# Attention and two MLPs on one core: program order on three engines before the first up product

## The chip, the core and the metric

One core of a Trainium2 chip runs the whole program. The time is device microseconds (us) of one execution; what counts is the median over several runs. TensorE (PE in the profile; PEld is its weight load), VectorE (DVE), ScalarE (ACT), GpSimd (POOL) and the DMA queues (SP and ACT issue on hardware queues, POOL on a software queue) each work through an instruction stream of their own, in order, and wait for one another by semaphores.

## What is computed

```python
def _attn_ref(q, k, v, s):                      # q, k, v: (4, 8, 576, 64); s: (4, 8, 576)
    scores = 1.0 / np.sqrt(D) * np.matmul(q, k.transpose(0, 1, 3, 2))
    cum = np.cumsum(np.maximum(s, 0.0), axis=-1)
    bias = -(cum[:, :, :, None] - cum[:, :, None, :])
    scores = np.where(causal, -1000000000.0, scores + np.minimum(bias, 0.0))
    attn = np.exp(scores - np.max(scores, axis=-1, keepdims=True))
    attn = attn / (np.sum(attn, axis=-1, keepdims=True) + 1e-09)
    return np.matmul(attn, v)
def reference(...):
    x = _attn_ref(q, k, v, s)                   # -> (2304, 512), all heads side by side
    x = np.maximum(x @ moe_w_in, 0.0) ** 2 @ moe_w_out          # 512 -> 2048 -> 512
    h = x @ moe2_w_in
    return np.maximum(0.01 * h, h) @ moe2_w_out
```

## The kernel before

The attention takes its 32 heads two at a time: 16 pairs, x = 0 to 15. A pair is worked in seven steps, k = 0 to 6, and the program's loop (line 810) counts them all as y = 7x + k. STEPS says what a step is: kind 0 (rows 0 to 255 of one head) at k = 0 and 1, kind 2 at k = 2 and 3, kind 3 at k = 4 and 5, kind 4 (the last 64 rows of both heads) at k = 6.

For one step the work goes through the engines in turn. TensorE makes the scores (`scores`, lines 457 and 469), two blocks ahead. VectorE adds the mask and takes the row's maximum (`maxima`, line 488). ScalarE makes the exponentials and their sums (`exponentials`, line 512). One or two steps later TensorE turns them (`flip`, line 527), and the turned blocks are copied out of PSUM by ScalarE (kinds 0 and 2, line 550) or by VectorE (kinds 3 and 4, line 548). TensorE multiplies them with v (`values`, line 569): the first 256 rows at k = 5, the rest at k = 3 of the next pair. ScalarE copies the product (`gather`, line 579).

The division by the sums comes in two portions for the first five pairs. `inverse` (lines 585 to 589) adds 1e-9 and takes the reciprocal on VectorE, and GpSimd spreads it over a tile `ex`; `spread` (line 604) turns that on TensorE; `scale` (lines 610 and 614) multiplies on VectorE. With k0 counted from the pair's own first step, the first portion has its inverse at k0 = 5 and its product at 9, the second its inverse at 8 and its product at 12.

Beside that, jobs come at fixed steps (`at_slot`): `load_bias`, `turn` (VectorE's transposes of the next pair's k and q, lines 427 and 430; from pair 5 on also a high and a low part, on ScalarE, line 431, and GpSimd, line 432), `last_rows` (GpSimd), `load_qk` (eight DMAs for two pairs, line 389), `load_v` (three DMAs and a GpSimd memset, lines 402 to 407), the loads of the attention's output as x of the first MLP (`up1_x`, with `split`: line 617 on ScalarE, line 618 on VectorE), and from step 11 on `load_w`: it reads 16 chunks of the first weight matrix (line 154, two `wst` buffers), each of which three steps later is put together from two words per element by ScalarE (lines 114 and 115), one step after that by VectorE (117 and 120) and GpSimd (122), then rounded by ScalarE (169) with the rest taken by GpSimd (172).

START[0] is step 35, the start of pair 5. From there on the first MLP's up products (`up1`, line 661) are laid between the attention's steps, and TensorE has enough to do. The ramp is what lies before: five pairs of attention alone. After the attention come the second half of the first MLP and the second MLP (line 877).

What sets the order. The program is written as one list of instructions. A planner then gives each engine its own order: it takes the instruction that is ready soonest by its own estimate, and the one written earlier among those that are ready. `in_order(start, engines)` (line 316) takes that freedom away: it chains what was written since `start` on each of the engines named, so that the engine works in the written order. `after(i)` (line 308) only says that what is written inside, on the engine of i, stands behind i in that engine's stream. Before the change TensorE alone is chained, from step 35 on (lines 812 and 871), and in the ramp only within each step (line 840). VectorE and ScalarE are free everywhere.

Of the kernel before, what the change touches and what calls it, by code (L numbers as in the profile page):

```python
# [23 lines left out]
def attention_then_two_mlps(  # L24
# [24 lines left out]
    nc = tc.nc  # L49
# [258 lines left out]
    def after(*instructions):  # L308

        stack = ExitStack()  # L310
        for i in instructions:
            if i is not None:
                stack.enter_context(tc.issue_after(i))
        return stack

    def in_order(start, engines):

        before = {}
        for i in nc.cur_bb.bb.instructions[start:]:
            if i.engine not in engines:  # L320
                continue
            if i.engine in before:
                tc.add_manual_dep(
                    i, before[i.engine].name,
                    mybir.DependencyInfo(mybir.DependencyClass.NoSync, mybir.DependencyReason.DATA),
                    reason="in_order")
            before[i.engine] = i
# [146 lines left out]
    def maxima(at, x, kind, e):  # L474

        p = pairs[x]  # L480
        if kind == 3 and x < PLAIN:
            t = f32(p.Y[:, 3 * e])
        else:
            t = at.tile([P, S], F32, tag="t", name="t", bufs=TB)
        m = at.tile([P, 16], F32, tag="m", name="m", bufs=TB + 1)

        def reduce(sc, msk, a, z, first, m):
            return nc.vector.tensor_tensor_reduce(t[:, a:z], sc, msk, -QK_SCALE, first, ALU.add, ALU.min, m).ins  # L488

        sc = p.sc[kind][e]  # L490
        if kind == 0:
            tiles = ((0, P, 0), (P, 3 * P, 1))
            for a, z, c in tiles:
                done = reduce(sc[:, a:z], mask[:, S - z + a:], a, z, 3.0e38, m[:, c:c + 1])
        elif kind == 4:
            tiles = ((0, S, 0),)
            reduce(sc[:, :S // 2], mask[:, :S // 2], 0, S // 2, 3.0e38, m[:, 1:2])
            done = reduce(p.sc[kind][1][:, :S // 2], mask4, S // 2, S, m[:, 1:2], m[:, 0:1])
        else:
            tiles = ((0, (kind + 1) * P, 0),)  # L500
            done = reduce(sc[:, :(kind + 1) * P], mask[:, S - (kind + 1) * P:], 0, (kind + 1) * P, 3.0e38, m[:, 0:1])
        if kind == 0 and e == 0:
            p.sums = at.tile([P, 16], F32, tag="sums", name="sums", bufs=4)
        T = {0: 0, 2: 2, 3: 3, 4: 4}[kind]
        p.t = t
        return t, m, tiles, p.sums, 2 * T + e, done

    def exponentials(t, m, tiles, sums, c0):

        for x, (a, z, c) in enumerate(tiles):  # L510
            s0 = c0 + 2 * x
            done = nc.scalar.activation(t[:, a:z], t[:, a:z], AF.Exp, bias=m[:, c:c + 1], scale=-1.0,  # L512
                                        accum_out=sums[:, s0:s0 + 1])
        return done.ins
# [59 lines left out]
    def gather(at, x, region, po):  # L574

        p = pairs[x]
        if region == 0:
            p.xo = at.tile([P, S], F32, tag="xo", name="xo", bufs=2)
        nc.scalar.activation(p.xo[:, :R] if region == 0 else p.xo[:, R:], po, AF.Copy)

    def inverse(at, x, a, z):

        p = pairs[x]
        cols = p.sums[:, 2 * a:min(2 * z, 9)]
        nc.vector.tensor_scalar(cols, cols, 1.0e-9, None, ALU.add)
        nc.vector.reciprocal(cols, cols)
        w = 2 * (min(z, 4) - a)
        p.ex = at.tile([P, w, 64], F32, tag="ex", name="ex")
        nc.gpsimd.tensor_copy(p.ex, p.sums[:, 2 * a:2 * a + w].unsqueeze(2).to_broadcast([P, w, 64]))
# [81 lines left out]
    def attention(at, mg, mx):  # L671

        n = len(STEPS)
        end = n * len(pairs)
        later = {}

        def at_slot(y, f, *args):
            later.setdefault(y, []).append((f, args))
# [58 lines left out]
        for x in range(len(pairs)):  # L737
            y = n * x
            if x + 1 < len(pairs):
                if x:  # L740
                    at_slot(y, load_bias, x + 1)
                late = 2 if x <= PLAIN else 0
                at_slot(y + 1 + late, turn, at, x + 1, "k")
                at_slot(y + 2 + late, turn, at, x + 1, "q")
                at_slot(y + 5, last_rows, x + 1)
            if x + 2 < len(pairs):
                if x and x % 2 == 0:
                    at_slot(y + 3, load_qk, at, x + 2)
                at_slot(y + 5, load_v, at, x + 2)

        def store(x):
            p = pairs[x]
            for e in range(2):
                c, d0 = divmod(p.h[e] * D, P)
                nc.sync.dma_start(xscr[c, d0:d0 + D, p.b * S:(p.b + 1) * S], p.xo[64 * e:64 * e + 64])
# [12 lines left out]
        def values_at(x, region):  # L768

            return 10 if region or ALONE <= x < len(pairs) - 1 else 5 if x < ALONE else 6  # L770
# [38 lines left out]
        live, anchors = {}, [None, None]  # L809
        for y in range(end + 14):  # L810
            x, st = divmod(y, n)
            if y == START[0]:
                fixed_from = len(nc.cur_bb.bb.instructions)
            if y < end:
                args = maxima(at, x, *STEPS[st])
                live[y] = args[0]
                behind = [args[-1], exponentials(*args[:-1])]
            fill(y, 0)
            tiled = len(nc.cur_bb.bb.instructions)
            for early in (True, False):  # L820
                for px in (x - 1, x):
                    if early or not 0 <= px < len(pairs):
                        continue
                    k0 = y - n * px
                    for region in range(2):
                        if k0 == values_at(px, region):
                            pairs[px].po[region] = values(px, region)
                for z in (y - LAG, y - 1):
                    zx, zs = divmod(z, n)
                    kind, e = STEPS[zs]  # L830
                    if early != (kind == 0 and zx < ALONE):
                        continue
                    if 0 <= z < end and (e or kind == 4) and (z == y - 1) == (kind == 3 and zx >= ALONE):
                        flip(at, zx, kind, [live.pop(i) for i in range(z - e, z + 1)])
            if y + 1 < end and STEPS[(y + 1) % n][1] == 0:
                last = len(KINDS) * x + KINDS.index(STEPS[st][0])
                while asked <= last + (2 if last + 2 < AHEAD else 1):
                    scores(asked // len(KINDS), KINDS[asked % len(KINDS)])
                    asked += 1
            in_order(tiled, (nc.tensor.engine,))  # L840
            divided = [i for i in nc.cur_bb.bb.instructions[tiled:] if i.engine == nc.tensor.engine][-1:]
            for px in (x - 1, x):
                if not 0 <= px < len(pairs):
                    continue
                k0 = y - n * px
                for region in range(2):
                    if k0 == values_at(px, region) + (region or px >= ALONE):
                        gather(at, px, region, pairs[px].po[region])
                final = 12 if px < ALONE else 13
                portions = ((9, 0, 2), (final, 2, 5)) if px < ALONE else ((final, 0, 5),)  # L850
                for when, a, b in portions:
                    if k0 == when:
                        scale(px, a, b)
                    if k0 == when - 4:
                        inverse(at, px, a, b)
                    if k0 == when - 1:
                        spread(px, a, b)
                if k0 == final:
                    store(px)
            with after(*divided):  # L860
                fill(y, 1)
            with after(*anchors, raw["last"]):
                for f, args in later.pop(y, ()):
                    f(*args)
            if y < end:
                anchors = behind
            fill(y, 2)
# [238 lines left out]
    with ExitStack() as stack:  # L1106
        b = open_pools(stack, ("b10", "bp2", "bp1", "bwst", "b00", "b01", "bop0", "bop1", "b11", "bwt"))
# [11 lines left out]
    with ExitStack() as stack:  # L1119
        b = open_pools(stack, ("c62", "cpa", "cpb", "cwst", "c17", "cy", "c543", "cp2", "cwa", "cwt"))  # L1120
# [17 lines left out]
    with ExitStack() as stack:  # L1138
        b = open_pools(stack, ("d01", "dpost", "dturn", "dpad", "dop0", "d00", "d11", "d10", "dop1"))
# [35 lines left out]
```

## Time and profile before

| | us |
|---|---|
| median of 3 runs (930.95 to 931.68) | 931.44 |
| the profiled execution | 932.79 |
| its span, first to last instruction | 931.0 |
| TensorE busy | 898.3 (96%) |
| VectorE busy | 705.7 (76%) |
| ScalarE busy | 577.7 (62%) |
| GpSimd busy | 179.9 (19%) |
| first up product (line 661) starts | 78.70 |

How to read it: a row of a timeline gives the start in the span, the length, engine, line, operation, output<-inputs, shape, and in brackets how long the engine had stood idle before and what ended that. [...] The profiled execution is 932.79 us long and its span 931.0, so 1.8 us lie around the span.

### The profile page before, as it was taken

What the parts mean: (1) busy time and instruction counts of PE and PEld (TensorE: products, weight loads), DVE (VectorE), ACT (ScalarE), POOL (GpSimd) and SP (SyncE); (2) the same over time, 40 slices, a digit from 0 to 9 for tenths busy, and PEclk for the clock granted to TensorE, in tenths of its full rate; (3) what the DMA queues carried; (4) which work ended last, traced back from release to release, by engine and by line L of the source; (5) the groups of instructions that cost most, each with busy time, mean ns of one, the idle gap of its engine ahead of it and who ended that gap; (6) DMA issues with size and microseconds to landing.
All of it is one profiled execution on the core that took longest, in us unless ns stands there. A gap on an engine that the chain in (4) does not pass through costs nothing.

```text
span 931.0 us, 16390 instructions
## 1 busy us (share of the span) xinstructions
PE 898.3 (96%) x5902; PEld 809.0 (87%) x5902; DVE 705.7 (76%) x1286; ACT 577.7 (62%) x1076; POOL 179.9 (19%) x290
## 2 busy tenths in 40 slices
PE   5878999999999999999999999999999999999997
PEld 3646777777777778999999999999999999999997
DVE  5888776876774267589897997787488697886964
ACT  4788876878886444365565556686577754444442
POOL 4357763344330001001112101001110000000000
PEclk9999999999999999999999999999999999999999
DMA  9776849778763377948649326668768575627303
GB/s 164 172 184 153 217 145 230 219 204 245 227 203 106 99 239 274 316 163 269 228 132 363 128 96 201 218 221 304 256 205 299 187 254 149 182 57 208 86 13 55
DMA packets 229569, 178.48 MB, mean 192 GB/s; under 512 B 139600, under 2 KB 206352, under 8 KB 229488
## 3 DMA queue, kind: packets, MB, share of 16 engines
q1 hardware_dynamic: 192568, 105.13, 41.7%
q10 hardware_dynamic: 27048, 38.16, 11.3%
q0 software_dynamic: 9872, 34.15, 10.5%
q8 instruction: 46, 0.75, 0.3%
q14 instruction: 35, 0.29, 0.1%
HBM read 111.25 MB, written 66.13 MB: 191 GB/s over the span
## 4 chain that ended last, share of the span: by engine, by line
PE 53%; issue 13%; DVE 6%; DMA 6%; POOL 1%; ACT 1%; POOLq 0%; ACTq 0%; DVEq 0%; SPq 0%
PE q L877 30%; PE h L661 16%; DVE op L984 3%; PE tr L569 2%; DMA gp<-gscr 2%; PE S L469 2%; PE tr L527 1%; PE S L457 1%; DMA gp<-qscr 1%; DMA wst<-in_moe_w_in_dram 1%; DMA qscr<-post 1%; DVE gp L978 1%; DMA wst<-in_moe_w_out_dram 1%; DVE wt L119 0%; POOL zscr L1046 0%
## 5 line engine op out<-in xcount | busy, mean ns | idle before, releaser
L877 PE MATMUL q<-op,w 128*128 128x384 f32 x3024 | 527.9, 335 | 4.0 <-DVE op L984 2.7
L877 PEld LDWEIGHTS q<-op,w 128*128 128x128 f32 x3024 | 523.7, 188 | 7.9 <-DVE op L984 5.0
L983 ACT ACTIVATE op<-gp 128x768 fp32r<-128x768 f32 x189 | 158.3, 846 | 152.3 <-PE q L877 128.4
L661 PE MATMUL h<-xs,w 128*128 128x512 f32 (+1 forms) x960 | 211.5, 374 | 1.2 <-ACT gs L640 0.8
L984 DVE TENSOR_TENSOR op<-gp,op 128x768 fp32r<-128x768 f32 x189 | 178.0, 953 | 40.6 <-ACT op L983 39.4
L661 PEld LDWEIGHTS h<-xs,w 128*128 128x128 f32 x960 | 163.6, 189 | 38.0 <-issue 6.0
L512 ACT ACTIVATE t<-t,m 128x256 f32<-128x256 f32 (+4 forms) x134 | 76.1, 569 | 44.1 <-DVE m L488 39.2
L488 DVE CUSTOM_DVE_ANT_0 t<-S,mask 128x128 f32<-128x128 f32 (+4 forms) x119 | 49.5, 460 | 43.3 <-PE S L469 28.2
L640 ACT ACTIVATE gs<-h 128x512 f32<-128x512 f32 (+1 forms) x80 | 43.8, 549 | 47.3 <-PE h L661 46.8
L185 POOL DMA_DIRECT2D wscr<-wt x48 | 26.6, 555 | 231.2 <-DVE wt L120 227.4
L950 DVE TENSOR_TENSOR post<-q,post 128x768 f32<-128x768 f32 (+1 forms) x55 | 51.6, 940 | 15.1 <-PE q L877 14.7
L469 PE MATMUL S<-Y 64*128 64x128 f32 (+3 forms) x324 | 42.9, 372 | 14.0 <-DVE Y L427 8.0
L930 ACT ACTIVATE post<-q 128x768 f32<-128x768 f32 (+1 forms) x56 | 43.8, 782 | 12.6 <-PE q L877 12.5
L114 ACT ACTIVATE wt<-wst 128x512 f32<-128x512 f32 x64 | 42.3, 661 | 12.2 <-DMA wst<-in_moe_w_in_dram 5.9
L569 PE MATMUL tr<-pT,v 128*64 128x320 f32 (+3 forms) x384 | 46.8, 387 | 2.5 <-ACT pT L550 2.0
L120 DVE SCALAR_TENSOR_TENSOR wt<-wst,wt 128x512 uint32<-128x512 uint32 x64 | 48.1, 753 | 0.9
L527 PEld LDWEIGHTS tr<-ident,t 64*128 64x128 f32 x720 | 28.6, 140 | 20.5 <-issue 11.3
L910 ACT ACTIVATE post<-post 128x768 f32<-128x768 f32 x36 | 30.4, 846 | 25.5 <-DVE post L950 25.4
L117 DVE TENSOR_SCALAR wt<-wt 128x512 uint32<-128x512 uint32 x64 | 31.7, 496 | 18.2 <-ACT wt L114 18.1
L569 PEld LDWEIGHTS tr<-pT,v 128*64 128x64 f32 x384 | 24.9, 137 | 23.1 <-issue 4.2
L115 ACT ACTIVATE wst<-wst 128x512 uint32<-128x512 uint32 x64 | 42.9, 670 | 2.7 <-DMA wst<-in_moe_w_out_dram 1.8
L198 DVE TENSOR_TENSOR w<-wq,w 128x512 fp32r<-128x512 f32 x49 | 33.3, 688 | 14.2 <-ACT w L197 13.9
(119 smaller groups left out, 943.7 us busy)
## 6 DMA issues: line engine op xcount, KB each, us to landing
gscr<-gs ACTq DMA_DIRECT2D x36, 512.0 KB
gp<-gscr SPq DMA_DIRECT2D x48, 384.0 KB
qscr<-post ACTq DMA_DIRECT2D x48, 384.0 KB
gp<-qscr SPq DMA_DIRECT2D x48, 384.0 KB
wscr<-wt POOLq DMA_DIRECT2D x48, 256.0 KB, 4.5
wst<-in_moe_w_in_dram SPq DMA_DIRECT2D x19, 512.0 KB
wst<-in_moe_w_out_dram SPq DMA_DIRECT2D x16, 512.0 KB
wst<-in_moe_w_out_dram POOLq DMA_DIRECT2D x16, 512.0 KB, 5.1
```

The lines of the kernel that those rows point to most:

```text
L120: nc.vector.scalar_tensor_tensor(t, hw, 0xC0000000, t, ALU.bitwise_and, ALU.bitwise_or)
L469: nc.tensor.matmul(p.sc[kind][e][:, a:z], qs[hs, T * P:(T + 1) * P], ks[hs, :z - a], start=(n == 0 and y == 0), stop=(n == len(tiles) - 1 ...
L488: return nc.vector.tensor_tensor_reduce(t[:, a:z], sc, msk, -QK_SCALE, first, ALU.add, ALU.min, m).ins
L512: done = nc.scalar.activation(t[:, a:z], t[:, a:z], AF.Exp, bias=m[:, c:c + 1], scale=-1.0, accum_out=sums[:, s0:s0 + 1])
L569: p.anchor = nc.tensor.matmul(po[64 * e:64 * e + 64, a:n], p.vr[:, c, e], rhs[e], start=(y == 0), stop=(y == len(mm) - 1), skip_group_chec ...
L640: done = nc.scalar.activation(g, h[:, :w], AF.Relu)
L661: nc.tensor.matmul(h[:, :w], win[fc][:, a, c * P:(c + 1) * P], xs[j, c][:, z, :w], start=(c == 0 and y == 0), stop=(c == KC - 1 and y == 2))
L877: i = nc.tensor.matmul(*args, skip_group_check=True, **kw).ins
L930: done = nc.scalar.activation(t[:, xs], acc, AF.Copy)
L950: done = nc.vector.tensor_tensor(t[:, xs], acc, t[:, xs], ALU.add)
L983: a = nc.scalar.activation(t[:, 0], src, AF.Copy)
L984: c = nc.vector.tensor_tensor(t[:, 1], src, f32(t[:, 0]), ALU.subtract)
```

## The change

Three edits in `attention`.

- The ramp is chained on all three engines. What is written from step 0 to step 34 keeps its written order on VectorE and ScalarE; TensorE's chain, which was from step 35 to the end, now begins at step 0.
- The inverse of the second portion (a > 0: pairs 0 to 4 alone have one) is written at k0 = 9 and not at 8, behind that step's maximum, and chained behind it.
- `load_v` for pair x + 2 is asked for at step 7x + 8 and not at 7x + 5, all through the attention.

```diff
@@ -746,7 +746,7 @@
             if x + 2 < len(pairs):
                 if x and x % 2 == 0:
                     at_slot(y + 3, load_qk, at, x + 2)
-                at_slot(y + 5, load_v, at, x + 2)
+                at_slot(y + 8, load_v, at, x + 2)
@@ -809,8 +809,10 @@
         live, anchors = {}, [None, None]
         for y in range(end + 14):
             x, st = divmod(y, n)
+            if y == 0:
+                fixed_from = len(nc.cur_bb.bb.instructions)
             if y == START[0]:
-                fixed_from = len(nc.cur_bb.bb.instructions)
+                in_order(fixed_from, (nc.vector.engine, nc.scalar.engine))
             if y < end:
                 args = maxima(at, x, *STEPS[st])
                 live[y] = args[0]
@@ -851,8 +853,9 @@
                 for when, a, b in portions:
                     if k0 == when:
                         scale(px, a, b)
-                    if k0 == when - 4:
-                        inverse(at, px, a, b)
+                    if k0 == (9 if a else when - 4):
+                        with after(behind[0] if a and y < end else None):
+                            inverse(at, px, a, b)
                     if k0 == when - 1:
                         spread(px, a, b)
```

## Rows read from the trace of the kernel before

**Rows 1.** Windows (columns as above): pairs 0 to 4, the steps behind, the rest.
```profile
10.69:22.63 11.94, 9.44 (x76) 6.29 (x74) 6.31 (x27) 7.56 (x23) 2.45 (x10) 0.86 0.99 180
22.63:34.78 12.15, 10.75 (x123) 7.71 (x121) 9.35 (x36) 8.77 (x26) 2.36 (x9) 1.00 0.63 166
34.78:49.43 14.65, 11.83 (x135) 8.19 (x132) 12.89 (x43) 11.31 (x31) 8.06 (x12) 1.00 0.91 183
49.43:64.81 15.38, 10.89 (x113) 7.72 (x113) 13.57 (x42) 12.58 (x33) 9.59 (x13) 1.00 0.60 171
64.81:78.48 13.67, 10.92 (x98) 6.97 (x100) 13.61 (x41) 10.70 (x29) 7.51 (x9) 0.88 0.82 174
78.48:92.00 13.52, 13.11 (x113) 9.57 (x110) 12.13 (x38) 11.80 (x31) 8.86 (x13) 1.00 0.58 162
92.00:925.00 833.00, 827.66 (x5249) 759.87 (x5248) 630.09 (x1052) 512.29 (x902) 133.87 (x205) 1.00 0.63 195
```

**Rows 2.** Timeline of TensorE in the ramp: step 3's last scores, and three of its waits.
```profile
15.33 0.51 PE L457 MATMUL h<-ag,last 128*128 128x288 f32 x1
17.84 1.07 PE L569 MATMUL tr<-pT,v 128*64 128x256 f32 x8 [2.01 <-ACT pT L550]
...
50.64 1.13 PE L469 MATMUL S<-Y 64*128 64x512 f32 x4 [1.40 <-DVE m L488]
...
66.05 2.01 PE L469 MATMUL S<-Y 64*128 64x512 f32 x4 [3.60 <-DVE m L488]
```

**Rows 3.** Windows, as rows 1: the two stretches at half clock.
```profile
18.40:21.80 3.40, 3.40 (x30) 2.58 (x28) 0.36 (x2) 2.10 (x6) 0.00 (x0) 0.50 1.09 194
...
66.10:69.60 3.50, 3.50 (x15) 1.55 (x17) 3.50 (x11) 3.50 (x12) 0.40 (x1) 0.51 1.13 191
```

**Rows 4.** Timeline of VectorE: pair 0's first inverse, and the transpose of pair 1's k.
```profile
12.92 0.17 DVE L585 TENSOR_SCALAR sums<-sums 128x4 f32<-128x4 f32 x1 [1.03 <-ACT t L512]
...
13.67 0.77 DVE L427 STREAM_TRANSPOSE Y<-kr 128x576 f32<-128x576 f32 x1
```

**Rows 5.** Timeline of ScalarE: pair 0's exponential of step 4 and the copies of step 3.
```profile
16.22 0.72 ACT L512 ACTIVATE Y<-Y,m 128x512 f32<-128x512 f32 x1 [0.57 <-DVE m L488]
...
16.94 0.85 ACT L550 ACTIVATE pT<-tr 128x384 f32<-128x384 f32 x2
```

**Rows 6.** Timeline of VectorE ahead of pair 4's first maximum.
```profile
61.91 1.23 DVE L585 TENSOR_SCALAR sums<-sums 128x5 f32<-128x5 f32 x1 [1.71 <-ACT t L512]
...
63.28 1.60 DVE L618 TENSOR_TENSOR xs<-xh,xs 128x512 fp32r<-128x512 f32 x1
64.81 0.28 DVE L488 CUSTOM_DVE_ANT_0 t<-S,mask 128x128 f32<-128x128 f32 x1
```

**Rows 7.** Timeline of GpSimd: three kinds of its long operations.
```profile
40.32 1.30 POOL L122 TENSOR_TENSOR wt<-wt,wst 128x512 uint32<-128x512 uint32 x1 [1.75 <-ACT pT L550]
...
61.84 2.50 POOL L172 TENSOR_TENSOR w<-wt,w 128x512 fp32r<-128x512 f32 x2
...
74.19 1.44 POOL L432 TENSOR_TENSOR Y<-yt,Y 128x576 fp32r<-128x576 f32 x1
```

**Rows 8.** Timeline of ScalarE: a weight word, and step 31's work.
```profile
45.65 0.68 ACT L114 ACTIVATE wt<-wst 128x512 f32<-128x512 f32 x1 [1.51 <-DMA wst<-in_moe_w_in_dram]
...
68.04 0.61 ACT L617 ACTIVATE xs<-xh 128x512 fp32r<-128x512 f32 x1
...
70.25 0.86 ACT L550 ACTIVATE pT<-tr 128x384 f32<-128x384 f32 x2
70.99 0.62 ACT L512 ACTIVATE t<-t,m 128x384 f32<-128x384 f32 x1
```

**Rows 9.** Timeline of SP's DMA issues: pairs 4 and 5, then a weight chunk.
```profile
33.37 3.03 SPq L389 DMA_DIRECT2D kr<-in_k_dram  x4
36.44 3.32 SPq L389 DMA_DIRECT2D qr<-in_q_dram  x4
41.65 0.38 SPq L154 DMA_DIRECT2D wst<-in_moe_w_in_dram  x1
```

## The prediction, made before the result was known

> **What bounds the kernel now.** I read the windows first, then the timelines of the engines in the ramp, and SP's at the end. The windows: one for each pair of the ramp and one for all that follows [rows 1]. From 92 us on TensorE is busy for 827.66 of 833.00, so 5.3 us of idle time are left there in all, while the five pairs from 10.69 to 78.48 take 67.79 us, in which TensorE is busy for 53.83. The work of TensorE after step 35 is the same in both kernels. So the change is worth what it does to the moment at which the first up product starts, and nearly nothing can be won or hidden behind it.
>
> Inside the ramp the limits differ. In pairs 0 and 1 no engine is full (VectorE 6.31 of 11.94 and 9.35 of 12.15): there it is latency, one engine waiting for the next. From pair 2 on the weight words are added, and VectorE is busy for 12.89, 13.57 and 13.61 of 14.65, 15.38 and 13.67 [rows 1]: 40.07 of 43.70. There VectorE is the bound, ScalarE follows with 34.59, and TensorE, at 33.64, has 10 us to spare. A gain in pairs 2 to 4 can be no more than the 3.63 us in which VectorE stands still; a loss can be much more.
>
> **Part 1: the order in pairs 0 and 1.** Two hoisted pieces do harm there, and the written order puts both back. First, VectorE waits 1.03 us for an exponential ahead of an inverse that nobody needs until step 8 [rows 4]; the maximum of step 2 stands behind that wait and the inverse's 0.3, so it can start at 11.89 and not at 13.22: 1.3 us. In the written order the inverse stands at step 5, where its sums are long done. Second, ScalarE makes the exponential of step 4 before the copies of step 3, and the copies run at 16.94 to 17.79 [rows 5]; TensorE stands idle for 2.01 us until they are there [rows 2]. In the written order the copies stand ahead of that exponential (0.7 us), the 1.3 are also saved, and k's transpose no longer stands ahead of step 3's maximum (0.7 more, [rows 4]). The copies could then start near 14.2, and what holds the values product is TensorE itself, which is at step 3's scores until 15.84 today [rows 2] and, with half a microsecond of its waits there gone, until about 15.3; the product starts there and not at 17.84: 2.5 us. Third, right behind the wait of 2.01 the granted clock was 0.50 for 3.4 us [rows 3], which is 1.7 us of work at full clock; the wait of 1.40 us [rows 2] was followed by no such stretch. I expect it to go: 2.5 + 1.7 = 4.2 us. If it stays, 2.5; if all that VectorE waits for here goes too, about 5.2. In pair 1 one wait of TensorE goes and another grows (the maximum of k = 1 now stands behind the two copies of kind 3, and not ahead of them): I take -0.5, between 0 and -0.9.
>
> **Part 2: the order in pairs 2 to 4.** Here the planner's order is dense, and the written one is less so. VectorE's work: 40.07, plus the words of step 32 (0.4 + 0.7, which the planner leaves until after 78.48), plus 0.4 for an inverse that today is done before 34.78: 41.5 us. To that come waits of the written order. Each is an estimate from the lengths that the timelines show for the operations between (a maximum 0.5 to 1.1, two copies of a turned block 0.8 on ScalarE and 1.2 on VectorE, a block of scores 1.3, turned blocks 0.5):
> - At step 14 the copies of kind 3 need TensorE's scores of step 13's end and 16 transposes, some 1.2 us behind the last maximum, with 0.6 of other work between: 0.6.
> - At step 31 VectorE's line 618 needs ScalarE's line 617, and ScalarE's written order puts step 31's exponential (0.7 with its sum), two copies (0.8) and then line 617 (0.6) behind VectorE's own maximum [rows 8]: 2.1 us in which VectorE can do nothing else. At step 28 the same costs 0.3, since 1.2 us of copies lie between.
> - Line 117 needs line 114, which ScalarE reaches behind the step's exponential, copies and gather: 1.5 us over steps 20, 27 and 32.
> - At step 30 `scale` needs the spread behind 1.3 us of scores: 0.3.
> - At step 34 the scores of pair 5 need GpSimd's line 432 (1.44) [rows 7], behind ScalarE's line 431: 0.7.
> The sum is 5.5, and 41.5 + 5.5 = 47.0. Some of VectorE's slow operations would fall into those waits: line 585 took 1.23 us, and not 0.17 as in [rows 4], while GpSimd was at line 172, and line 618 took 1.60 [rows 6, 7]. I take 0.5 off: 46.5 against 43.70, a loss of 2.8. The bounds: if VectorE waits no longer in all than today, 41.5 + 3.6 = 45.1, a loss of 1.4; if none of that is absorbed, two more such collisions come (2.1) and GpSimd's line 432 stands behind one of its lines 122 (1.3), 50.4, a loss of 6.7.
>
> [...]
>
> **Part 3: the moved inverse.** At 60.2 VectorE waits 1.71 us for an exponential ahead of the second inverse of pair 3, which then takes 1.23, and pair 4's first maximum, whose scores were ready, stands behind all that and line 618 until 64.81 [rows 6]; TensorE waits 3.60 us for that maximum's successor, and the clock is at 0.51 behind it [rows 2, 3]. With the inverse behind step 30's maximum this wait is gone. I don't count it again: it is part of VectorE's 3.63 us. Cost of the move: the spread comes at k0 = 11, two steps later, and GpSimd's 0.4 us copy fits between: nothing, as long as GpSimd isn't held by a DMA.
>
> **Part 4: load_v.** Its buffer's last reader is the values product written at 7x + 3, so at 7x + 8 neither SP nor GpSimd's memset has to wait for it, and three DMAs of about 0.6 us each move behind the bias load. v is needed at 7x + 19. Nothing on the path; it takes a block away from SP's queue. TensorE's own chain adds next to nothing, since it is in order within each step already.
>
> **Behind step 35.** VectorE and ScalarE have fewer words left over. From 78.48 to 92 TensorE is idle for 0.41 us [rows 1]; I take -0.3.
>
> **Sum.** -4.2 - 0.5 + 2.8 - 0.3 = -2.2: the profiled execution 932.79 becomes 930.6, and against the median 931.44 it is 929.2.
>
> **The rivals.**
> - *It cancels.* The written order's waits come in full: -4.7 + 3.3 (none absorbed) + 1.3 (GpSimd's order) - 0.3 = -0.4: 931.0. For it: VectorE and ScalarE are both near full, and each now waits in place. Against: the planner's order waits too, at every inverse.
> - *Slower: weights late.* ScalarE now stops at line 114 until its chunk is there, with every later exponential behind it, and so VectorE and TensorE. Already today it waits 1.51 us so [rows 8], for a chunk asked for at 41.65, four us before [rows 9]. Its buffer comes free when line 122 is done (41.62, [rows 7]); in the written order that is near 35, and ScalarE wants it near 42, so 3 us are to spare. If the eight issues of pairs 4 and 5 (6.4 us, [rows 9]) stand between, the chunk lands at 35 + 6.4 + 4.0 = 45.4, a stall of 3.4; and a stall of that size has brought the half clock, in which four score products took 2.01 us and not 1.13 [rows 2], some 1.5 us over the stretch. -2.2 + 4.9 = +2.7: 934.1. It decides from an issue more than 3 us after the buffer is free. Against: these issues wait for pair 2's bias only, and could be through by then.
> - *More is won.* VectorE waits no more than today in pairs 2 to 4 (loss 1.4): -3.6, and with pair 0 at its bound -4.6: 927.3.
> - *The order is free again after step 35,* and the planner's streams there can come out otherwise; with 5.3 us of idle time in all [rows 1], I give it 1 us either way, inside the range.
>
> **How the numbers follow.** Forecast (929.2, on its own 928 to 930.5): 0.33. More won: 0.16. Cancels: 0.29. Weights late: 0.22. A measurement of this kernel can tell about 0.2%, 1.9 us, from no change. Faster: all of "more is won" (0.16) and 0.28 of the forecast, 0.44. Same: the rest of the forecast (0.05) and 0.26 of "it cancels", 0.31. Slower: the rest of that (0.03) and "weights late" (0.22), 0.25. The range takes in "more is won" with the planner's 1 us (926.3) and "weights late" (934.1).
>
> **What would show it.** Right: pair 1's first maximum near 18.4 and not 22.63, no half clock near 20 us; VectorE idle in pairs 2 to 4 longer than 3.6 us, with the longest wait ahead of line 618 near step 31; line 585 no longer waiting for an exponential; first up product near 76.7. Wrong: a wait of ScalarE for `wst` of over 2 us, half clock still at the start, or a first up product after 78.7.

## The result: slower by 1.0%, and the profile after

| | before | after |
|---|---|---|
| median, us | 931.20 (6 runs, 930.30 to 933.04) | 940.50 (6 runs, 939.17 to 943.97) |
| ratio, with its 95% interval | | 1.0098 (1.0084 to 1.0112) |
| profiled execution, us | 932.79 | 941.01 |
| its span, us | 931.0 | 939.2 |
| first up product starts, us | 78.70 | 85.02 |

The forecast was 929.2 in a range of 926.3 to 934.2. The time lies outside it, on the slow side.

The windows of the kernel after, cut at the first maximum of each pair as in [rows 1]. Columns, there as here: stretch, its length, busy time of PE, PEld, DVE, ACT and POOL with their instructions, granted TensorE clock (1.00 is the full clock, 0.50 half of it), DMA share, GB/s.

```profile
10.68:18.54 7.86, 7.86 (x64) 4.83 (x62) 6.05 (x24) 6.50 (x22) 2.46 (x10) 1.00 0.98 178
18.54:30.16 11.62, 10.01 (x114) 7.04 (x111) 9.62 (x37) 7.66 (x25) 1.51 (x6) 1.00 0.82 197
30.16:46.30 16.14, 12.54 (x119) 8.59 (x118) 14.79 (x45) 13.09 (x35) 7.44 (x12) 0.95 0.87 190
46.30:62.22 15.92, 13.25 (x134) 9.24 (x130) 13.43 (x43) 12.66 (x33) 8.73 (x13) 0.94 0.51 153
62.22:84.28 22.06, 13.57 (x101) 8.60 (x103) 15.39 (x44) 14.00 (x37) 14.19 (x18) 0.72 0.81 171
84.28:92.00 7.72, 7.72 (x52) 5.54 (x50) 5.65 (x21) 3.44 (x12) 0.85 (x3) 0.68 0.27 99
92.00:933.00 841.00, 834.68 (x5315) 765.46 (x5312) 636.41 (x1066) 517.04 (x914) 136.91 (x208) 1.00 0.62 194
```

Set beside [rows 1], the 8.2 us of the span come apart like this. Pairs 0 and 1 take 19.48 and not 24.09: 4.6 won. Pairs 2 and 3 take 32.06 and not 30.03: 2.0 lost. Pair 4 takes 22.06 and not 13.67: 8.4 lost. From step 35 to the end there are 854.92 us and not 852.52: 2.4 lost. Step 28 still came 2.6 us earlier than before; step 35 came 5.8 later. The lead is gone by step 29's scores, which start at 66.08 and before the change at 66.05 [rows 2]. From there to step 35 it is 18.20 us against 12.43. The question is what happened between 62 and 84 us.

TensorE's waits there, in its timeline. A row is start, length, engine, line, operation, and in brackets the idle time ahead of it and what ended that.

```profile
66.08 2.08 PE L469 MATMUL S<-Y 64*128 64x512 f32 x4 [3.15 <-DVE m L488]
...
78.50 0.59 PE L527 MATMUL tr<-ident,t 64*128 64x64 f32 x11 [2.45 <-ACT xo L579]
80.02 0.80 PE L469 MATMUL S<-Y 64*128 64x128 f32 x4 [0.92 <-DVE m L488]
82.59 1.22 PE L469 MATMUL S<-Y 64*128 64x128 f32 x8 [1.78 <-POOL Y L432]
```

The first is step 29: the scores of the next steps need the tile `S` that step 29's maximum reads, and wait 3.15 us for it. The kernel before waited there too, for 3.60 us [rows 2]. The second is step 33, whose turned blocks need the tile `tr` that ScalarE's gather (line 579) empties (2.45). The last is step 34: the scores of pair 5 need the low part of its q (GpSimd's line 432; 1.78). VectorE's timeline shows what stood ahead:

```profile
64.09 1.38 DVE L618 TENSOR_TENSOR xs<-xh,xs 128x512 fp32r<-128x512 f32 x1
65.40 0.28 DVE L488 CUSTOM_DVE_ANT_0 t<-S,mask 128x128 f32<-128x128 f32 x1
...
69.24 0.42 DVE L610 TENSOR_TENSOR xo<-xo,tr 128x256 f32<-128x256 f32 x1 [1.81 <-PE tr L604]
...
73.69 0.69 DVE L618 TENSOR_TENSOR xs<-xh,xs 128x512 fp32r<-128x512 f32 x1 [2.13 <-ACT xs L617]
74.30 0.77 DVE L430 STREAM_TRANSPOSE yt<-kr 128x576 f32<-128x576 f32 x1
...
75.58 0.77 DVE L430 STREAM_TRANSPOSE yt<-qr 128x576 f32<-128x576 f32 x1
...
77.62 1.64 DVE L120 SCALAR_TENSOR_TENSOR wt<-wst,wt 128x512 uint32<-128x512 uint32 x1
...
84.28 0.29 DVE L488 CUSTOM_DVE_ANT_0 t<-S,mask 128x128 f32<-128x128 f32 x1 [1.82 <-PE S L469]
```

And ScalarE's, from step 31's end:

```profile
75.10 0.69 ACT L431 ACTIVATE Y<-yt 128x576 fp32r<-128x576 f32 x1 [1.45 <-DVE yt L430]
75.69 0.61 ACT L169 ACTIVATE w<-wt 128x512 fp32r<-128x512 f32 x1
76.21 0.65 ACT L114 ACTIVATE wt<-wst 128x512 f32<-128x512 f32 x1
76.77 0.66 ACT L115 ACTIVATE wst<-wst 128x512 uint32<-128x512 uint32 x1
77.32 0.71 ACT L512 ACTIVATE Y<-Y,m 128x512 f32<-128x512 f32 x1
...
78.02 0.42 ACT L579 ACTIVATE xo<-tr 128x320 f32<-128x320 f32 x1
78.34 0.68 ACT L431 ACTIVATE Y<-yt 128x576 fp32r<-128x576 f32 x1
```

What shows here is one list. The turning of pair 5's k and q (lines 430 and 431) stands at steps 31 and 32, behind all that is written before it. VectorE stands still for line 617 (2.13), turns k, and only then can ScalarE make its high part; then come four more of its operations (75.69 to 78.02), and the gather for which TensorE waits is behind them. GpSimd is in no written order: its order is the planner's. q's high part is done at 79.02, and GpSimd makes a line 122 before it comes to q's low part, which starts at 81.12 and ends at 82.5:

```profile
77.25 1.46 POOL L172 TENSOR_TENSOR w<-wt,w 128x512 fp32r<-128x512 f32 x1
...
79.87 1.29 POOL L122 TENSOR_TENSOR wt<-wt,wst 128x512 uint32<-128x512 uint32 x1
81.12 1.42 POOL L432 TENSOR_TENSOR Y<-yt,Y 128x576 fp32r<-128x576 f32 x1
```

The same lines in the kernel before (its GpSimd row is in [rows 7]). VectorE:

```profile
66.40 0.77 DVE L430 STREAM_TRANSPOSE yt<-kr 128x576 f32<-128x576 f32 x1
70.00 0.77 DVE L430 STREAM_TRANSPOSE yt<-qr 128x576 f32<-128x576 f32 x1
```

And ScalarE in the kernel before:

```profile
69.67 0.69 ACT L431 ACTIVATE Y<-yt 128x576 fp32r<-128x576 f32 x1
71.59 0.69 ACT L431 ACTIVATE Y<-yt 128x576 fp32r<-128x576 f32 x1
72.21 0.44 ACT L579 ACTIVATE xo<-tr 128x320 f32<-128x320 f32 x1
```

There the planner turned k at 66.40, 1.6 us after pair 4's first maximum; after the change it is 12.1 us after it. The line ends 6.9 us later on the clock (82.54 and 75.63), though pair 4 began 2.6 us earlier.

Then the clock. Three stretches at half clock, as windows:

```profile
44.90:48.20 3.30, 3.30 (x29) 2.85 (x30) 2.07 (x9) 2.31 (x7) 2.10 (x4) 0.50 0.74 196
65.30:72.10 6.80, 6.02 (x28) 2.84 (x30) 4.38 (x18) 3.65 (x10) 3.91 (x4) 0.50 1.04 198
79.00:89.10 10.10, 7.40 (x55) 5.89 (x54) 6.08 (x24) 5.11 (x17) 5.58 (x10) 0.50 0.47 141
```

That is some 20 us, where [rows 3] has two stretches of 3.4. The last one reaches over the first up products: from 84.28 to 92.00 the clock is 0.68, so by estimate 7.72 x 0.32 = 2.5 us of work at full clock are missing, about the 2.4 us lost behind step 35.

### The profile page after: what moved, and what is told of

Read it like the earlier page. It is cut to its first block, busy times and chain, and to the rows that moved or that the text cites. A ratio compares the mean times of both kernels' runs of the same rounds, so it can differ in the third digit from the quotient of the medians.

```text
span 939.2 us, 16387 instructions
## 1 busy us (share of the span) xinstructions
PE 903.6 (96%) x5902; PEld 812.2 (86%) x5902; DVE 709.0 (75%) x1286; ACT 577.1 (61%) x1076; POOL 179.3 (19%) x290
## 3 DMA queue, kind: packets, MB, share of 16 engines
q0 software_dynamic: 9872, 34.15, 10.5%
## 4 chain that ended last, share of the span: by engine, by line
PE 57%; issue 8%; DMA 3%; DVE 3%; ACT 1%; POOL 1%; POOLq 0%; ACTq 0%; DVEq 0%; SPq 0%
PE q L880 43%; PE h L661 11%; PE tr L569 1%; DVE op L987 1%; DMA gp<-zscr 1%; PE S L469 1%; PE tr L527 1%; DMA wst<-in_moe_w_out_dram 1%; DMA xh<-xscr 0%; PE S L457 0%; POOL zscr L1049 0%; ACT w L197 0%; DMA gscr<-gs 0%; DMA wb<-wscr 0%; DVE gp L981 0%
## 5 line engine op out<-in xcount | busy, mean ns | idle before, releaser
L548 DVE COPY pT<-tr 128x512 f32<-128x512 f32 (+1 forms) x64 | 33.9, 550 | 15.1 <-PE tr L527 14.9
```

## The experiments

The theory before the first runs: the written order is what costs in pair 4, with VectorE and ScalarE waiting for each other and TensorE's clock falling behind the waits (theory A of the first four). Its rivals: the two moved pieces cost (B), and an early ramp is taken back by what it then waits for (C). Ratios are against runs of the kernel before on the same chip; e1 to e4 have 10 runs each, e5 to e8 only 4, e9 to e13 12. Pair 4 is from the first maximum of step 28 to that of step 35, in the profiled execution.

| run | what differs from the changed kernel | ratio (95%) | pair 4, us | first up product, us |
|---|---|---|---|---|
| before | | | 13.67 | 78.70 |
| after | | 1.0098 (1.0084 to 1.0112) | 22.06 | 85.02 |
| e1 | no order, the moves alone | 1.0036 (1.0015 to 1.0057) | 14.06 | 78.65 |
| e2 | order ends at step 28 | 0.9995 (0.9974 to 1.0016) | 16.97 | 77.86 |
| e3 | order ends at step 14 | 0.9986 (0.9966 to 1.0006) | 15.94 | 73.96 |
| e4 | lines 617, 618 left out | 1.0045 (1.0029 to 1.0061) | 21.22 | 84.09 |
| e5 | ScalarE free | 1.0092 (1.0065 to 1.0119) | 19.38 | 86.25 |
| e6 | VectorE free | 1.0114 (1.0071 to 1.0156) | 18.34 | 86.16 |
| e7 | weight words left out | 1.0100 (1.0073 to 1.0126) | 18.88 | 86.09 |
| e8 | maxima from step 28 left out | 1.0074 (1.0045 to 1.0102) | 23.91 | 84.37 |
| e9 | turning of pair 5 left out | 1.0004 (0.9983 to 1.0025) | 17.17 | 78.07 |
| e10 | turning written two steps earlier | 1.0033 (1.0016 to 1.0051) | 19.66 | 82.82 |
| e11 | order ends at 28, no moves | 0.9996 (0.9977 to 1.0016) | 17.49 | 77.31 |
| e12 | order ends at 28, load_v back | 0.9988 (0.9969 to 1.0006) | 16.93 | 77.65 |
| e13 | order ends at 28, turning alone pinned | 1.0010 (0.9999 to 1.0021) | 17.69 | 78.44 |

### Which part costs: the moves, or the order, and from where

e1 takes VectorE and ScalarE out of the change (and begins TensorE's chain at step 35 again):

```diff
-            if y == 0:
+            if y == START[0]:
                 fixed_from = len(nc.cur_bb.bb.instructions)
-            if y == START[0]:
-                in_order(fixed_from, (nc.vector.engine, nc.scalar.engine))
```

> Only the two moves (inverse at k0 = 9, load_v at 7x + 8); no chain in the ramp, as before. Theory A (the written order of pair 4 is what costs: VectorE and ScalarE wait for each other at steps 28 to 34, TensorE stands still for over 2 us three times, and half clock follows): within 2 us of before, 931. Theory B (the moves cost: the later inverse holds scale and spread, or the later load_v holds weights and GpSimd): most of the 9 us stays, 937 or more.

e2 and e3 keep everything but end the order of VectorE and ScalarE early:

```diff
-            if y == START[0]:
+            if y == 28:                     # e3: 14
                 in_order(fixed_from, (nc.vector.engine, nc.scalar.engine))
```

> The changed kernel, but the chain on VectorE and ScalarE ends at step 28, so pairs 0 to 3 keep the written order and pair 4 is the planner's again. Theory A: step 28 stays near 62.2 (64.8 before), pair 4 takes some 13.7 us and not 22.1, first up product near 76, total 931.2 - 2.6 = 928.6. Theory B: pair 4 stays long, 937 or more.

> The chain on VectorE and ScalarE ends at step 14: only pairs 0 and 1 keep the written order. Theory A: step 14 near 30.2 (34.8 before), and from there 43.7 us to step 35 as before: 931.2 - 4.6 = 926.6. Theory B: 937 or more. Theory C (a late start of pair 2 in the planner's order is bound by the weights' DMAs, so that the 4.6 us are given back in pairs 2 to 4): 931.

e4 leaves the two lines of `split` out of the order (`loose` is a set of names that `in_order` passes over):

```diff
-            if i.engine not in engines:
+            if i.engine not in engines or i.name in loose:
                 continue
...
-        split([t[:, z] for z in range(2)], xf)
+        loose.update(i.name for i in split([t[:, z] for z in range(2)], xf))
```

> The changed kernel, but lines 617 and 618 (x's high and low part, at steps 28 and 31) stand outside the chain on both engines; everything else is chained. Theory A with these two lines as the main cause: the wait of 2.1 at step 31 and the 3.2 of TensorE at step 29 go, and half clock from 65.3 to 72.1 with them: 940.5 - 2.1 - 1.4 - 3.4 = 933.6. If steps 32 to 34 are the main cause (high and low part of k and q on ScalarE and GpSimd behind the weight words): 938.

Measured: ending the order at step 28 (e2) takes the whole loss away, so the loss is in the order of steps 28 to 34. TensorE's own chain runs from step 0 in e2 and e3 as well, so it costs nothing that shows. But e2 doesn't win the 2.6 us that theory A gave it. Its pair 4, in the planner's order, takes 16.97 us and not 13.7, so a lead of 4.3 us at step 28 is 0.8 at the first up product. In its trace ScalarE stands still for 2.69 us, until 75.68, for a weight chunk, with a gather behind it for which TensorE waits 1.44. Leaving the split out (e4) takes about half of the loss away, but pair 4 is still 21.22 us long; its 937.2 is near the 938 that was expected if steps 32 to 34 are the main cause. The first up product is only 0.9 us earlier there; its trace also has less half clock, 13.7 us in three stretches and not 20.5, by estimate a difference of at most 3.4 us of work (half of 6.8). The moves alone (e1) come out 0.36% slower; their ramp is the old one (first up product 78.65), and the loss lies behind it. e11 and e12 come back to that.

e3 is at 931.17, the number of theory C and not the 926.6 of A, but not by C's mechanism: pairs 2 to 4 give nothing back. Its first up product comes 4.7 us earlier than before, and yet the median shows no more than 0.14%, within the uncertainty. Its TensorE timeline:

```profile
84.08 0.96 PE L661 MATMUL h<-xs,w 128*128 128x512 f32 x3 [1.30 <-DVE xs L618]
85.79 2.12 PE L661 MATMUL h<-xs,w 128*128 128x512 f32 x8 [0.75 <-DVE xs L618]
89.40 0.66 PE L457 MATMUL S<-Y,last 128*128 128x288 f32 x3 [0.65 <-DVE m L488]
```

Of the 4.7 us, 2.7 go into waits for x and for a maximum before 90 us. So an early end of the ramp is partly given back: 2.05 us because x is not ready, 0.65 for the maximum. The other 2 us are seen in this execution (last q product 924.05, before 926.13), and the median doesn't tell them from nothing.

### One engine, the words, the maxima

e5 and e6 change the engines named in the order: `(nc.vector.engine,)` or `(nc.scalar.engine,)`. e7 puts lines 114, 115, 117, 120 and 169 of the weight words into `loose`. e8 puts the maxima of step 28 and later there:

```diff
+                from_here = len(nc.cur_bb.bb.instructions)
                 args = maxima(at, x, *STEPS[st])
+                if y >= 28:
+                    loose.update(i.name for i in nc.cur_bb.bb.instructions[from_here:] if i.engine == nc.vector.engine)
```

> The changed kernel with VectorE's written order alone; ScalarE is free for the planner in the whole ramp. Theory A1 (VectorE's written order costs: a maximum stands behind the copies of the step before and behind line 618, and holds the score banks that TensorE waits for): still slow, pair 4 over 20 us long, 938 to 941. Theory A2 (ScalarE's written order costs: lines 114, 115, 169 and 431 stand ahead of an exponential and a gather that TensorE waits for): pair 4 back to 14 to 16 us, 931 to 934. Theory A3 (each waits for the other, so that either order alone costs little): 933 to 936.

> The changed kernel with ScalarE's written order alone; VectorE is free for the planner. A1: pair 4 back to 14 to 16 us, 931 to 934. A2: still slow, pair 4 over 20 us, 938 to 941. A3: 933 to 936. In each case the gain of pair 0 (pair 1 from 18.5 us) should be partly lost if it is VectorE's order that brings it.

> The changed kernel, but the weight words (lines 114, 115, 117, 120, 169) are left out of the written order, on VectorE and ScalarE both. A2: steps 31 to 34 get shorter (no half clock near 79 us, the wait of 2.45 us at 76 us gone), pair 4 some 16 us, 933 to 935. A1: step 29's maximum is as late as in the changed kernel, the wait of about 3 us at 63 us stays, pair 4 still 19 us or more, 937 to 940.

> The changed kernel, but from step 28 on VectorE's maxima alone (line 488 and its like) are left out of the written order. A1: step 29's maximum comes near 63 and not at 65.4 us, no half clock behind 65 us, first up product 3 to 5 us earlier than in the changed kernel, 933 to 937. A2: little changes, since ScalarE's list still holds the exponential and the gather, 938 to 941.

Measured: none recovers more than the uncertainty allows. The first up product comes at 84.4 to 86.3 us in all four, wherever pair 4 began. A1, A2 and A3 each fall as they were put: no one engine, and neither the words nor the maxima, carries the loss. What e5 and e6 do show is that either order alone brings most of pair 0's gain: pair 1's first maximum comes at 19.13 and 18.92, where both give 18.54 and the kernel before has 22.63. They say little on pair 4, since with one engine free pairs 2 and 3 get longer already (step 28 at 67.2 and 67.4 us, 62.22 in the changed kernel); so it is with e7 (66.47). e8 was the telling one. Step 29's maximum was early as A1 wanted (step 28 began at 59.72, and TensorE had no wait over 0.33 us between 60 and 63), and the time went into another wait of TensorE:

```profile
76.94 0.59 PE L529 MATMUL tr<-ident,t 64*128 64x64 f32 x11 [2.15 <-ACT xo L581]
81.94 1.22 PE L471 MATMUL S<-Y 64*128 64x128 f32 x8 [3.93 <-POOL Y L434]
```

(Lines are shifted by 2: L434 is line 432.) The wait for pair 5's q grew to 3.93. That line ends at 81.6 us in e4, 83.0 in e5, 84.7 in e6, 83.6 in e7, 81.9 in e8, 82.5 after; 75.6 before, 75.4 in e1, 74.4 in e2, 71.0 in e3. What the slow kernels have in common, and the others not, is that line 430 or 431 of pair 5 stands in its written place. By itself this shows nothing, since the quick ones have no written order at all behind step 28. It made theory T.

### The turning of pair 5

e9 leaves it out of the order (`begin` is the place at which `turn` starts to write):

```diff
         nc.scalar.activation(hi, yt, AF.Copy)
         nc.gpsimd.tensor_tensor(lo, yt, f32(hi), ALU.subtract)
+        loose.update(i.name for i in nc.cur_bb.bb.instructions[begin:])
```

e10 keeps all in the order and writes the turning two steps earlier:

```diff
-                late = 2 if x <= PLAIN else 0
+                late = 2 if x <= PLAIN and x != 4 else 0
```

> The changed kernel, but the turning of pair 5's k and q (and of later pairs: lines 430 and 431 and GpSimd's 432) is left out of the written order. Theory T (every slow kernel so far has line 430 or 431 of pair 5 in its written place at steps 31 and 32; the q half of line 432 ends at 81.6 to 84.7 us there, at 71 to 75.6 us in the quick ones, and step 34's scores follow it): line 430 of k moves to before 68 us, line 432 of q ends before 77, the first up product comes at 78 to 81 us instead of 85.0, 932 to 936. Theory A (VectorE and ScalarE wait for each other all through steps 28 to 34, whatever the turning does): line 432 comes earlier, but step 35 stays past 82 us, 937 to 940.

> The changed kernel with the turning of pair 5 written two steps earlier (steps 29 and 30, not 31 and 32), all of it in the written order. T: line 432 of q ends some 4 us earlier (near 78), no wait of TensorE for it, first up product at 80 to 82 us, 934 to 937. A: the same work stands ahead of other maxima instead, first up product within 1 us of 85.0, 939 to 941.

Measured: e9 is at 1.0004, the whole loss gone with two lines of two engines, everything else in written order to step 35. All that T forecast for it came true. e10, which frees nothing, is at 1.0033: two thirds of the loss gone, though its first up product, 82.82, is later than the 80 to 82 that T gave. GpSimd's timeline in e9 (L435 is line 432 there):

```profile
69.32 1.77 POOL L435 TENSOR_TENSOR Y<-yt,Y 128x576 fp32r<-128x576 f32 x1 [1.89 <-ACT Y L434]
...
73.03 1.50 POOL L435 TENSOR_TENSOR Y<-yt,Y 128x576 fp32r<-128x576 f32 x1 [0.35 <-ACT Y L434]
```

And TensorE's longest waits in e9 ahead of the first up product:

```profile
64.88 2.08 PE L473 MATMUL S<-Y 64*128 64x512 f32 x4 [2.98 <-DVE m L492]
75.69 0.59 PE L531 MATMUL tr<-ident,t 64*128 64x64 f32 x11 [0.67 <-ACT xo L583]
```

The wait at step 29 is still there, with a half clock (64.44 to 71.27; the clock is 0.80 over pair 4), and yet this kernel is level with the one before. The waits for the gather (2.45) and for q (1.78) are 0.67 and none, and there is no half clock at 79 (the clock is 1.00 from 78.35 to 92.00). VectorE's timeline in e9 (L433 is line 430, L492 line 488) shows where the rest comes from:

```profile
66.15 0.77 DVE L433 STREAM_TRANSPOSE yt<-kr 128x576 f32<-128x576 f32 x1
...
70.20 0.77 DVE L433 STREAM_TRANSPOSE yt<-qr 128x576 f32<-128x576 f32 x1
...
74.85 0.69 DVE L120 SCALAR_TENSOR_TENSOR wt<-wst,wt 128x512 uint32<-128x512 uint32 x1
75.46 0.68 DVE L492 CUSTOM_DVE_ANT_0 Y<-S,mask 128x512 f32<-128x512 f32 x1
```

Both transposes stand in time in which VectorE stands still in the changed kernel: its wait for the spread at step 30 is 1.12 and not 1.81, that for line 617 at step 31 is 1.44 and not 2.13. Step 33's maximum comes 10.6 us behind step 29's scores, and 13.1 in the changed kernel: 2.5 us, 0.95 of it because line 120 takes 0.69 and not 1.64. Step 35 comes 13.5 us behind those scores and not 18.2: another 2.2 us, behind step 33. So of the 8.4 us that pair 4 lost, e9 gives back 4.9 (17.17 against 22.06). The other 3.5 it still has, hidden by a start that is 3.6 us earlier: 2.5 of them lie between step 28 and step 29's scores (3.70 us, 1.24 in the kernel before), where the wait of 2.98 stands, and 1.0 behind. The changed kernel has 3.86 us in that place.

In e10 q's low part ends at 73.9 and the wait for it is gone too, but the gather still stands behind the words, as TensorE's timeline in e10 shows:

```profile
78.60 0.90 PE L527 MATMUL tr<-ident,t 64*128 64x64 f32 x11 [2.79 <-ACT xo L579]
```

with a half clock from 77.29 to 84.12 (the clock is 0.90 from 82.08 to 92.00). These two are what its timeline still shows ahead of the first up product; no run takes them apart.

e13 asks the other way round: is the place of the turning enough by itself? Behind step 28 only the operations around it are chained:

```diff
+            if y == START[0]:
+                in_order(fixed_from, (nc.vector.engine, nc.scalar.engine), pinned)
```

where `pinned` holds lines 617 and 618 of step 31, 430 and 431 of pair 5, and step 32's maximum, exponential and gather (nine operations; the expectation counts eight).

> Written order to step 28 on VectorE and ScalarE as in the run that ended it there (ratio 0.9995); behind that only the eight instructions around pair 5's turning keep their written order: on VectorE line 618 of step 31, line 430 for k, step 32's maximum, line 430 for q; on ScalarE line 617, line 431 for k, step 32's exponential and gather, line 431 for q. T1 (the place of the turning is enough by itself): line 432 of q ends past 79 us, first up product past 81, 936 to 940. T2 (it costs only together with the words and copies that stand ahead of it in the full order): line 432 of q ends by 76, first up product at 77 to 79.5, 930 to 934.

Measured: 1.0010, so T2, with every number inside what T2 gave. The planner brought all the pinned operations forward together, and q's low part ended at 72.7. Its place among these few costs nothing that 0.2% would show; it costs behind the whole list of steps 28 to 31. (This kernel's profiled execution, 936.21, was 2.8 us above its median.) In that execution something else came last. ScalarE in e13:

```profile
75.15 0.66 ACT L114 ACTIVATE wt<-wst 128x512 f32<-128x512 f32 x1 [4.18 <-DMA wst<-in_moe_w_in_dram]
```

And TensorE in e13:

```profile
77.39 1.11 PE L532 MATMUL tr<-ident,Y 64*128 64x64 f32 x15 [3.62 <-ACT xo L584]
```

ScalarE stood 4.18 us for a weight chunk, with an exponential and a gather behind. This is the mechanism of the rival "weights late", at 75 us and not near 42, in a kernel whose steps 31 and 32 were early, as in e2.

### The moves

e11 and e12 are e2 with `inverse` and `load_v` both back, and with `load_v` alone back:

> The kernel before with VectorE's and ScalarE's written order up to step 28 alone: neither the inverse nor load_v is moved. Theory C (the moves themselves cost some 0.3% behind the ramp, as the run with the moves alone was 1.0036 of before, and the order to step 28 with the moves 0.9995): the order alone wins what the moves took, 927 to 929, ratio 0.996 to 0.998. Rival C0 (the moves cost nothing of themselves; what comes behind the ramp is the planner's other order, which each kernel draws anew): 930 to 932, ratio 0.999 to 1.001.

> Written order to step 28, the inverse moved, load_v in its old slot. C with load_v as the cause (its DMAs come later and the planner's list behind the ramp is another): as the run without either move, 927 to 929. C with the inverse as the cause: as with both moves, 930 to 932. C0: 930 to 932, and not distinct from the others.

Measured: 0.9996 and 0.9988, beside 0.9995 with both moves. The three aren't distinct, so C as it was put there falls: with the order to step 28, the moves have no price that shows within 0.2%. What made e1 slower by 0.36% isn't settled; the planner lays its free instructions otherwise in each kernel, and no run holds its order behind step 35 fixed. No run here beats the kernel before by more than its interval: e12 and e3 come nearest.

## Why the prediction was wrong, point by point

**Pairs 0 and 1 (Part 1): right in size, and in cause in the main.** Forecast -4.7, measured -4.6: 4.1 in pair 0 (TensorE's idle time there fell by 2.50, its busy time, with the half clock gone, by 1.58) and 0.5 in pair 1. Pair 1's first maximum is at 18.54 (forecast 18.4), no half clock stands near 20 us (1.00 from 10.68 to 30.16), pair 0's inverse (16.28) runs without a wait. The copies of step 3 came at 14.79 and the product at 16.07, 0.6 and 0.8 us later than I put them. That two hoisted pieces each cost a share of their own is not borne out: e5 and e6 put one engine back each, and each has most of the gain.

**Pairs 2 to 4 (Part 2): this is the step that failed.** Forecast +2.8, at most +6.7; measured 54.12 against 43.70, +10.4. VectorE's work rose by 3.5 (43.61 against 40.07), where I had 1.0; its standing still rose by 6.9 (10.5 against 3.6), where I had 1.9. With pair 5's turning out of the order (e9) the same three pairs take 48.78, +5.1: so 5.3 of the 7.6 us that I was off belong to the place of the turning, and 2.3 to the rest, TensorE's wait at step 29 above all. The terms one by one:
- Line 618 behind 617 at step 31, forecast 2.1, measured 2.13. The mechanism and its size were right.
- "At step 34 the scores of pair 5 need GpSimd's line 432 (1.44), behind ScalarE's line 431: 0.7." This is the term that was wrong. I priced its last operation and not its place. Lines 430, 431 and 432 are a chain over three engines, which the planner began at 66.40 and the written order at 74.30, and [rows 7] shows its last link alone. I hadn't read where the kernel before does lines 430 and 431, nor what stands ahead of them in the written lists. e9 shows that this place carries the loss, e10 that two thirds of it go with a move of two steps, e13 that the place costs only behind the rest of the list. VectorE's last wait, ahead of step 35's maximum, was 1.82 for my 0.7. The item of the upper bound that has line 432 behind a line 122 (1.3) came true: q's low part began 2.1 us behind the end of its high part.
- At step 30 `scale` waited 1.81, forecast 0.3. Its spread stood behind scores at half clock: four of them took 2.08 us, near the 2.01 of the kernel before at half clock, and not 1.13 [rows 2]; and these scores stood behind TensorE's wait of 3.15.
- At step 28 the wait of line 618 was small, as I said (it ran at 64.09, right behind line 617), but its own length was 1.38, and step 29's maximum stood behind it and the copies. TensorE's wait of 3.15 for that maximum was nowhere in my sum, though [rows 2] has 3.60 at the same place: Part 3 took VectorE's wait ahead of it away, and so it went, but TensorE's stayed. VectorE wasn't late there; it did other work first. I counted what VectorE loses, not who waits for each of its results.
- The collisions: two of VectorE's operations in pair 4, line 618 with 1.38 and line 120 with 1.64, took 0.69 elsewhere, so 1.6 us more. The kernel before had collisions of its own in pairs 2 to 4: what lines 117, 120, 585 and 618 took there beyond their usual lengths (0.41, 0.69, 0.17 and 0.69) adds up to 4.9 us before and 5.4 after (4.9 and 4.2 without line 120, which had the longest collision of pair 4). So collisions explain 0.5 of the rise of 3.5. All 15 of these operations that took over 0.1 us more than usual in pairs 2 to 4 (6 before, 9 after) began while GpSimd was at its line 122, 172 or 432; two others that began so, within 0.06 us of its end, took their usual length. Line 120 began at 77.62, beside GpSimd's line 172, which ended at 78.71, and ended 0.55 us later.

**The half clock: counted only in a rival.** I took it to go from pair 0 and for the rest priced it in "weights late" alone, 1.5 us. It came back at TensorE's waits of 1.15, 3.15 and 2.45, for 20 us in all. In the ramp before, each of TensorE's two waits of over 2 us (2.01 and 3.60) had 3.4 us of it behind it [rows 2, 3], so a case with waits of that size had to carry a price for it, the forecast too.

**The moved inverse and load_v (Parts 3 and 4): nothing, as forecast,** as far as e2, e11 and e12 can tell (0.2%); why e1 was slower stays open. Line 585 no longer waits for an exponential: VectorE's timeline shows no wait ahead of any of its nine in the ramp; before, one waited 1.03 us and one 1.71 [rows 4, 6].

**Behind step 35: forecast -0.3, measured +2.4,** about what the half clock over the first up products takes. Another premise is weaker than I put it: that the change is worth what it does to the first up product, with 1 us either way behind it. e1 has the first up product of the kernel before and is 3.4 us slower; e3 has it 4.7 us earlier and is not clear of the kernel before. So even a ramp as forecast needn't have given 929.2.

**The rivals.** "More is won" and "it cancels" lie on the quick side of what was measured (927.3, by the way, is the middle of that rival's -3.6 and -4.6, not either of them). "Weights late" was the one on the slow side, with 934.1, and it didn't happen: in the changed kernel none of ScalarE's waits of over 1 us in the ramp is for a chunk. Its shape (ScalarE held, TensorE waiting behind, the half clock behind that) was what happened, with the turning in the place of the weights. The weights themselves held ScalarE in two of the quicker kernels, near 75 us (2.69 in e2, 4.18 in e13). What I had named as signs of being wrong split: the first up product after 78.7 came true, the other two didn't. Of the signs of being right, the longest wait of VectorE in pairs 2 to 4 was the one ahead of line 618 at step 31, as I said.

## What to carry to other kernels

In this kernel the written order was only as good as the place of its rarest job. Where a planner is taken away, follow each job that isn't part of the regular step over all its engines, from its written place to its first reader, and compare that with where the planner had it. An engine's sum of work and waits didn't price the order here; ask for every result on the list who waits for it, and what of the list stands ahead of it. And a chain for which only the last link was read in the profile isn't priced.

## What I hadn't expected of the hardware

In these runs the length of a wait of TensorE alone didn't tell whether the half clock came with it, nor for how long. In the changed kernel it came at a wait of 1.15 us (from 44.82, for 3.4 us), not at 1.61 and 1.56 (near 20 and 32 us), for 6.8 us at 3.15, and for 10.2 us at 2.45, behind which two more waits (0.92 and 1.78) stood. In e9 the same wait of 1.56 near 32 us did come with it, from 33.72 for 3.4 us (the clock is 0.89 over pair 2); there a wait of 2.98 came with 6.8 us of it, and in e10 one of 3.38 with 3.4.
